# Low bits of the first layer's weights on VectorE, the second group's inversion alone on GpSimd, conversions placed behind its norms, ten weight loads ahead

## The chip, the cores and the metric

The kernel runs on one core of one Trainium2 chip. The metric is the device time of one execution in microseconds (us). Its engines are TensorE (PE; its weight loads are a row of their own, PEld), VectorE (DVE), ScalarE (ACT), GpSimd (POOL) and SyncE (SP), which here only issues DMA transfers. Each engine works through its own queue in order; semaphores tie the queues together.

## The reference

A linear attention with the delta rule, one time step after another, and then two feed-forward layers:

```python
k_n = k / (norm(k) + 1e-06)                    # q, k, v: 4 x 8 heads x 768 steps x 48
for t in range(768):
    y[t] = q[t] @ state
    state += beta[t] * outer(k_n[t], v[t] - k_n[t] @ state)
x = y as 3072 x 384
h = x @ w_in                                   # 384 x 2048
x = where(h >= 1, h, where(h <= -1, 0, (h + 1)**2 / 4)) @ w_out
h = x @ w_in2
out = max(h, 0)**2 @ w_out2
```

All in float32; the second layer's inputs and weights come with it, of the same sizes.

## The kernel before

**Tiling.** The 768 steps are cut into 24 chunks of 32. Per chunk the recurrence becomes matrix work: Gram matrices of keys and queries (`gram`), the inverse of a triangular matrix per head (`tri`), and products with the running state (`chunk_steps`: `ks`, `tr`, `qs`, `ku`, `pu`, `xt`). The triangular inverses are made for groups of chunks at a time, 2, 4, 4, 4, 4, 4, 2 of them. `tri` transposes the Gram tiles (`begin`, tile gm), computes norms and factors (`pre`), does a chain of dependent steps of two instructions each (`step`, L418 and L419, tiles t and tx), and transposes the result back (`end`, L422). For the first two groups only the two 16 x 16 diagonal halves are inverted in this way, in 14 steps; `joined` makes the block between them with PE products, for which `rows` (L452) transposes part of tx into a tile d (first group) or ld (second).

**Weights.** Products of 32-bit floats are made of parts: a weight is split into a rounded high part and a low part. The weights come as 64-bit values and are converted on the chip, in 32 tiles of 128 x 384 per layer. A conversion has these instructions: ACT scales the upper words into `wt` (L173, "prelu" in the code), the low bits are taken from the lower words into `wl` (L165), DVE joins the two (L183, "join"), ACT casts the high part (L194), and the low part is the difference of the two (L198, "difference"). For the first layer, L165 runs on POOL, and L198 on POOL for the input weights (i = 0) and on DVE for the output weights (i = 1). `wt` has 3 buffers and `wl` has 4. The raw weights of the first layer land in the buffers that later hold the converted ones. The second layer's conversions (on DVE, L165 too) are spread over the blocks of the first layer.

**Order.** The first part (loads, the first group's inversion, the second group's Gram tiles) is in the order in which the code writes it, on all engines. From `tc.manual_schedule(engines=ENGINES)` on only PE keeps the written order; the other queues are ordered by the scheduler, with its own cost model, under the limits of data, buffers and `issue_after`. The feed-forward stream then runs block after block (9 blocks of 2 or 3 chunks, 16 tiles f each, two slots per f), with a product h for tile f and the products into acc for tile f - 2. The attention work of the next chunks, the inversions and the conversions are put into slots of that stream (`put`, `put_a`, `HEAD`). `end1` and `rows1` of the second group are in slot 3 of the first block. SP issues transfers in order; a transfer whose buffer is not free holds those behind it.

**Names in the steps.** gp: Gram tiles of a group, later the inverse; l, ld, z: tiles of the second group's joining; kqt, kv: keys and queries, keys and values; raw: weights as they come; u, tr, ks, yy, xt: products of a chunk; sps and st: the running state in PSUM and SBUF; gh, gl: high and low part of the activated h. `first1(n)` issues the raw loads up to the n-th; `ahead` (L227 to L229) issues more as conversions go on; `more_w1` issues the next conversions.

Of the kernel before, what the change touches and what calls it, by code (L numbers as in the profile page):

```python
# [8 lines left out]
F32 = mybir.dt.float32  # L9
# [16 lines left out]
def kernel(  # L26
# [38 lines left out]
    EAGER = 26  # L65
# [6 lines left out]
    HEAD = 8  # L72
# [87 lines left out]
    def convert_stages(key, box, eng=None):  # L160
        eng = eng or nc.vector

        def low():
            box["t"] = tmp("wl", WL)
            eng.tensor_scalar(  # L165
                box["t"].bitcast(I32), box["raw"][:, :, 0].bitcast(U32), 2.0 ** -29, 7.0,
                ALU.mult, ALU.min,
            )

        def s0():  # L170
            raw = box["raw"] = raws.pop(key)
            t = box["w"] = tmp("wt", WT)
            nc.scalar.activation(  # L173
                t, raw[:, :, 1].bitcast(F32), AF.Prelu, scale=2.0 ** -112, alpha=2.0 ** 32
            )
            if eng is not nc.vector:
                low()

        def s1():
            if eng is nc.vector:  # L180
                low()
            t, bits = box["w"].bitcast(I32), box["t"].bitcast(I32)
            nc.vector.scalar_tensor_tensor(  # L183
                bits, t, 3, bits, ALU.logical_shift_left, ALU.bitwise_or
            )

        return [s0, s1]


    def part_stages(key, box):  # L190
# [5 lines left out]
        def s4():  # L196
            hi, lo = weight(i, f)
            (nc.vector if i else nc.gpsimd).tensor_sub(lo, box["t"], hi.bitcast(F32))  # L198

        return convert_stages(key, box, nc.gpsimd) + [s3, s4]  # L200
# [3 lines left out]
    def weight_items(w):  # L204
# [5 lines left out]
        def item(x):  # L210
            _, f, i = keys[x]
            box = {}
            if w == 0:
                r = part_stages(keys[x], box)
# [4 lines left out]
            r[1] = lambda: (s1(), ahead(x + 1 + RAW))  # L219
# [121 lines left out]
    def tri(n, eng, halves=False):  # L341
# [34 lines left out]
        def gamma2():  # L376
            nc.vector.scalar_tensor_tensor(r, g, -1.0, bet[:, n, :], ALU.mult, ALU.mult)
            nc.vector.tensor_mul(g, g, bet[:, n, :])
# [66 lines left out]
    def joined(n):  # L445
# [5 lines left out]
        def rows():  # L451
            nc.vector.transpose(d.rearrange("p q j -> p j q"), tx[:, 0:T2])  # L452
# [246 lines left out]
    with tc.manual_schedule():  # L699
# [3 lines left out]
        first1(2)  # L703
# [6 lines left out]
        first1(EAGER // 2)  # L710
        load_kv(HEADS)
        first1(EAGER)
# [22 lines left out]
        masks = [gram(0, 1, 2, late=2, eng=G)]  # L735
        cross_gram(0, 1)
        masks.append(gram(1, 1, 2, late=2, eng=G))
        for c in range(HEADS):
            save0(c)
        go([gram(c, late=2, eng=G) for c in range(GFIRST[1], GFIRST[2])])  # L740
        go(steps)
# [6 lines left out]
        begin()  # L748
    ENGINES = {mybir.EngineType.PE}
    with tc.manual_schedule(engines=ENGINES):  # L750
# [3 lines left out]
        go(pre)  # L754
# [5 lines left out]
        for fs in [[k0, t0], [k1], [q0, p0], [t1_], [q1], [x0], [p1], [x1]]:  # L760
            go(fs)
            more_w1(2)
# [45 lines left out]
        put(0, 3, *later(end1, rows1))  # L808
# [117 lines left out]
```

## Time and profile before

| | |
|---|---|
| median of 3 runs | 1098.58 us (1098.39 to 1100.24) |
| profiled execution | 1098.07 us |
| its span, first to last instruction | 1096.4 us |
| granted TensorE clock, mean | 0.976 of full speed |
| PE busy | 988.2 us, 90% of the span |
| DVE, ACT, POOL busy | 594.7, 513.4, 357.0 us |

The profile is one execution as the hardware profiler recorded it. A busy time counts the instructions of an engine, waits inside an instruction included; "idle before" and the name behind an arrow tell how long an engine had nothing running before an instruction and which work ended that. A matmul of 32-bit operands appears as two instructions or more. The chain of waits follows the last instruction back to what released it, step by step. The clock is that of TensorE alone, as a share of 2.4 GHz.

### The profile page before, as it was taken

Reading aid. Unit: us, or ns where it says so; the run is one execution under the profiler, and the core shown is the slowest. Engines: PE = TensorE matmul, PEld = TensorE weight load, DVE = VectorE, ACT = ScalarE, POOL = GpSimd, SP = SyncE. Lnnn points to the kernel's source line nnn. Section 1 sums busy time; section 2 is a strip of 40 time slices with the busy share of each in tenths; the row PEclk is TensorE's granted clock in tenths of the full one; section 3 lists DMA queues with packets and bytes.
Section 4 is the critical chain, followed back from the end, with each engine's and each line's share of the span. In section 5 each row is a group of like instructions: output and inputs, shape, how many; then the busy total and the mean of one; then the engine's idle time right before and its main releaser. Section 6 shows DMA issues by size and latency. Waiting matters only on the chain.

```text
span 1096.4 us, 34188 instructions
## 1 busy us (share of the span) xinstructions
PE 988.2 (90%) x14952; PEld 943.5 (86%) x14952; DVE 594.7 (54%) x1080; ACT 513.4 (47%) x1083; POOL 357.0 (33%) x474
## 2 busy tenths in 40 slices
PE   3340599899999999999999999999999999999998
PEld 3330588789989998999999999999999999999998
DVE  5662347767657666666755467743434343434333
ACT  3362246555555555565665666433333333333332
POOL 5989208618503921841940023210101010101000
PEclk9985799999999999999999999999999999999999
DMA  9910042534344144250212132301001010000000
GB/s 288 319 50 0 31 132 85 153 90 132 88 125 146 46 153 118 68 149 28 67 31 74 32 96 78 101 1 44 27 17 44 1 45 1 22 1 23 1 22 22
DMA packets 36054, 80.96 MB, mean 74 GB/s; under 512 B 4545, under 2 KB 18369, under 8 KB 35905
## 3 DMA queue, kind: packets, MB, share of 16 engines
q1 hardware_dynamic: 35904, 78.78, 23.6%
q8 instruction: 117, 1.92, 0.7%
q14 instruction: 33, 0.26, 0.1%
HBM read 63.03 MB, written 15.73 MB: 72 GB/s over the span
## 4 chain that ended last, share of the span: by engine, by line
PE 78%; DVE 7%; POOL 4%; issue 4%; DMA 3%; ACT 3%; SPq 0%; DVEq 0%; ACTq 0%; POOLq 0%
PE acc L574 34%; PE h L574 34%; POOL wl L165 2%; PE tr L505 2%; DMA raw<-in_w_dram 2%; PE sps L536 2%; PE g L289 2%; PE yy L491 2%; PE yy L525 1%; DVE g L603 1%; DMA kqt<-in_kq_dram 1%; PE ks L491 1%; POOL w L198 1%; ACT r L599 1%; DVE r L601 1%
## 5 line engine op out<-in xcount | busy, mean ns | idle before, releaser
L574 PE MATMUL h<-xh,w 128*128 128x384 f32 (+1 forms) x1632 | 319.6, 331 | 4.3 <-ACT g L600 3.4
L574 PEld LDWEIGHTS h<-xh,w 128*128 128x128 f32 x1632 | 270.9, 189 | 10.1 <-ACT g L600 2.5
L612 DVE TENSOR_TENSOR gl<-g,gh 128x384 fp32r<-128x384 f32 (+1 forms) x272 | 170.0, 625 | 144.1 <-ACT gh L611 141.6
L611 ACT CAST gh<-g 128x384 fp32r<-128x384 f32 (+1 forms) x272 | 134.5, 495 | 209.1 <-DVE g L603 103.8
L574 PE MATMUL h<-xl,w 128*128 128x384 f32 (+1 forms) x816 | 178.6, 327 | 1.1 <-DVE xl L562 1.1
L574 PE MATMUL acc<-gh,w 128*128 128x384 f32 (+1 forms) x864 | 166.6, 328 | 0.8 <-ACT gh L611 0.8
L606 DVE TENSOR_TENSOR g<-r 128x384 f32<-128x384 f32 x128 | 71.3, 557 | 157.8 <-ACT r L605 157.8
L574 PE MATMUL acc<-w,gh 128*128 128x384 f32 x768 | 155.5, 337 | 1.6 <-DVE e L619 1.6
L605 ACT ACTIVATE r<-h,zero 128x384 f32<-128x384 f32 x128 | 74.5, 582 | 166.7 <-PE h L574 166.7
L574 PEld LDWEIGHTS h<-xl,w 128*128 128x128 f32 x816 | 140.5, 189 | 1.7 <-DVE xl L562 1.7
L574 PEld LDWEIGHTS acc<-gh,w 128*128 128x128 f32 x864 | 135.2, 188 | 6.4 <-ACT gh L611 1.0
L574 PEld LDWEIGHTS acc<-w,gh 128*128 128x128 f32 x768 | 136.3, 188 | 1.9 <-ACT gh L611 1.9
L599 ACT ACTIVATE r<-h,one 128x384 f32<-128x384 f32 (+1 forms) x144 | 78.4, 545 | 84.3 <-PE h L574 83.4
L603 DVE TENSOR_TENSOR g<-g,r 128x384 f32<-128x384 f32 (+1 forms) x144 | 90.9, 631 | 42.7 <-ACT r L602 41.5
L601 DVE TENSOR_SCALAR r<-r 128x384 f32<-128x384 f32 (+1 forms) x144 | 64.8, 450 | 80.9 <-ACT r L599 80.0
L661 POOL CAST xh<-x2r 128x1152 fp32r<-128x1152 f32 x8 | 9.5, 1188 | 293.5 <-PE h L574 246.1
L418 POOL TENSOR_TENSOR t<-tx,gm 128x58 f32<-128x58 f32 (+9 forms) x164 | 94.8, 578 | 15.4 <-DVE tx L397 3.7
L419 POOL TENSOR_TENSOR tx<-tx,t 128x58 f32<-128x58 f32 (+9 forms) x164 | 95.5, 582 | 12.6
L574 PE MATMUL acc<-gl,w 128*128 128x384 f32 (+1 forms) x432 | 90.3, 317 | 0.0
L574 PE MATMUL acc<-w,gl 128*128 128x384 f32 x384 | 88.0, 337 | 0.0
L265 POOL TENSOR_TENSOR kv<-kv,nt 128x384 f32<-128x384 f32 x24 | 22.3, 931 | 201.3 <-DMA kv<-in_kv_dram 80.8
L602 ACT ACTIVATE r<-r 128x384 f32<-128x384 f32 (+1 forms) x144 | 70.5, 490 | 21.4 <-DVE r L601 20.8
(107 smaller groups left out, 1017.0 us busy)
## 6 DMA issues: line engine op xcount, KB each, us to landing
raw<-in_w_dram SPq DMA_DIRECT2D x64, 384.0 KB, 4.8
kqt<-in_kq_dram SPq DMA_DIRECT2D x88, 192.0 KB, 3.8
kv<-in_kv_dram SPq DMA_DIRECT2D x24, 384.0 KB, 3.1
w2f<-wl SPq DMA_DIRECT2D x32, 192.0 KB, 3.7
w2r<-w2f SPq DMA_DIRECT2D x16, 384.0 KB, 3.0
x2r<-x SPq DMA_DIRECT2D x8, 576.0 KB, 4.4
out_dram<-e SPq DMA_DIRECT2D x24, 192.0 KB, 2.0
x<-e SPq DMA_DIRECT2D x18, 192.0 KB, 2.5
```

The source lines that it names most:

```text
L418: eng.tensor_mul(t, by.to_broadcast(shape), of.to_broadcast(shape))
L419: eng.tensor_add(rest, rest, t)
L491: per_bh(lambda b, h, p, pd: nc.tensor.matmul(o[p, h], kqt[c][pd, b // 2, h, x * T:(x + 1) * T], st[pd, b // 2, h], start=h == 0, stop=x = ...
L574: nc.tensor.matmul(o, *((r, l) if swap else (l, r)), **flags)
L599: marks[0] = nc.scalar.activation(r, h, AF.Relu, bias=one)
L601: marks[1] = nc.vector.tensor_scalar(r, r, 2.0, 0.5, ALU.min, ALU.mult)
L602: nc.scalar.activation(r, r, AF.Square)
L603: nc.vector.tensor_add(g, g, r)
L605: marks[0] = nc.scalar.activation(r, h, AF.Relu, bias=zero)
L606: marks[1] = nc.vector.tensor_mul(g, r, r)
L611: nc.scalar.copy(ghi, g)
L612: nc.vector.tensor_sub(glo, g, ghi.bitcast(F32))
```

## The change

Four edits. (1) The low bits (L165) of the first layer's weights go from POOL to DVE, into the same stage as the join; of the differences (L198) of the input weights, those of the first 12 conversions go to DVE as well, the others stay on POOL. (2) `more_w1` calls of the hand-written part come under `issue_after` the last of the second group's factor instructions (the second line of `gamma2`), three steps of the conversion pipeline after each group of chunk products instead of two; the first part of that group's `pre` moves ahead, into the fully manual part. (3) The first two weights are no longer loaded ahead of the keys and values; ten are loaded ahead, and each conversion issues the load of the tenth after it, instead of 26 ahead and three. (4) The Gram tiles of the second group come ahead of the remaining ones of the first, `end1` and `rows1` move from slot 3 to 4, and `HEAD` from 8 to 10.

```diff
     LAG = 2
-    EAGER = 26
+    EAGER = 10
+    ALONE = 12
...
-    HEAD = 8
+    HEAD = 10
...
-    def convert_stages(key, box, eng=None):
-        eng = eng or nc.vector
-
-        def low():
-            box["t"] = tmp("wl", WL)
-            eng.tensor_scalar(
-                box["t"].bitcast(I32), box["raw"][:, :, 0].bitcast(U32), 2.0 ** -29, 7.0,
-                ALU.mult, ALU.min,
-            )
-
+    def convert_stages(key, box):
         def s0():
             raw = box["raw"] = raws.pop(key)
             t = box["w"] = tmp("wt", WT)
             nc.scalar.activation(
                 t, raw[:, :, 1].bitcast(F32), AF.Prelu, scale=2.0 ** -112, alpha=2.0 ** 32
             )
-            if eng is not nc.vector:
-                low()
 
         def s1():
-            if eng is nc.vector:
-                low()
-            t, bits = box["w"].bitcast(I32), box["t"].bitcast(I32)
+            raw, t = box["raw"], box["w"].bitcast(I32)
+            box["t"] = tmp("wl", WL)
+            bits = box["t"].bitcast(I32)
+            nc.vector.tensor_scalar(
+                bits, raw[:, :, 0].bitcast(U32), 2.0 ** -29, 7.0, ALU.mult, ALU.min
+            )
             nc.vector.scalar_tensor_tensor(
                 bits, t, 3, bits, ALU.logical_shift_left, ALU.bitwise_or
             )
...
-    def part_stages(key, box):
+    def part_stages(x, key, box):
...
         def s4():
             hi, lo = weight(i, f)
-            (nc.vector if i else nc.gpsimd).tensor_sub(lo, box["t"], hi.bitcast(F32))
-
-        return convert_stages(key, box, nc.gpsimd) + [s3, s4]
+            (nc.vector if i or x < ALONE else nc.gpsimd).tensor_sub(lo, box["t"], hi.bitcast(F32))
+
+        return convert_stages(key, box) + [s3, s4]
...
             s1 = r[1]
-            r[1] = lambda: (s1(), ahead(x + 1 + RAW))
+            r[1] = lambda: (s1(), ahead(x + 1 + (RAW if w else EAGER)))
...
         def gamma2():
             nc.vector.scalar_tensor_tensor(r, g, -1.0, bet[:, n, :], ALU.mult, ALU.mult)
-            nc.vector.tensor_mul(g, g, bet[:, n, :])
+            return nc.vector.tensor_mul(g, g, bet[:, n, :])
...
         nc.sync.dma_start(bet, beta)
-        first1(2)
         for c in range(GROUPS[0], KQ):
             load_kq(c)
         for c in range(KG):
             load_kg(KQ + c)
         for c in range(HEADS):
             load_kv(c)
-        first1(EAGER // 2)
+        first1(EAGER)
         load_kv(HEADS)
-        first1(EAGER)
...
         go(pre)
-        masks = [gram(0, 1, 2, late=2, eng=G)]
-        cross_gram(0, 1)
-        masks.append(gram(1, 1, 2, late=2, eng=G))
         for c in range(HEADS):
             save0(c)
         go([gram(c, late=2, eng=G) for c in range(GFIRST[1], GFIRST[2])])
+        cross_gram(0, 1)
+        masks = [gram(c, 1, 2, late=2, eng=G) for c in range(HEADS)]
         go(steps)
         for c in range(HEADS):
             value(c)
...
         begin, pre, steps, end1 = tri(1, G, True)
         begin()
+        ins = go(pre[:-2])
+        behind[0] = lambda: tc.issue_after(ins.ins)
     ENGINES = {mybir.EngineType.PE}
     with tc.manual_schedule(engines=ENGINES):
         for f in (ld0, dld0):
             for c in range(HEADS):
                 f(c)
-        go(pre)
+        go(pre[-2:])
...
         for fs in [[k0, t0], [k1], [q0, p0], [t1_], [q1], [x0], [p1], [x1]]:
             go(fs)
-            more_w1(2)
+            more_w1(3)
...
-        put(0, 3, *later(end1, rows1))
+        put(0, 4, *later(end1, rows1))
         for c in range(GROUPS[1]):
             put_a(0, HEAD - 3 + 3 * c, lambda c=c: ld1(c))
             put_a(0, HEAD - 2 + 3 * c, lambda c=c: dld1(c))
```

What it does to POOL's queue, around the second group's first steps. L418 and L419 are one step (t, then tx), L165 the low bits (wl), L198 the difference. Before:

```order
L198 TENSOR_TENSOR w07_1110<-wl_1093,w07_1110 128x384
L418 TENSOR_TENSOR t_732<-tx_80,gm_576 128x28
L165 TENSOR_SCALAR wl_1158<-raw_143 128x384
L198 TENSOR_TENSOR w08_1153<-wl_1115,w08_1153 128x384
L165 TENSOR_SCALAR wl_1187<-raw_145 128x384
L419 TENSOR_TENSOR tx_80<-tx_80,t_732 128x2x14
L165 TENSOR_SCALAR wl_1197<-raw_147 128x384
L165 TENSOR_SCALAR wl_1261<-raw_149 128x384
L198 TENSOR_TENSOR w09_1192<-wl_1158,w09_1192 128x384
L418 TENSOR_TENSOR t_736<-tx_80,gm_576 128x52
```

Now (L411 and L412 are the step):

```order
L376 TENSOR_TENSOR gm_544<-gm_544,st2_547 128x2x16x16
L385 TENSOR_TENSOR tx_80<-gm_544,st1_546 128x2x16x16
L411 TENSOR_TENSOR t_700<-tx_80,gm_544 128x28
L412 TENSOR_TENSOR tx_80<-tx_80,t_700 128x2x14
L411 TENSOR_TENSOR t_704<-tx_80,gm_544 128x52
L412 TENSOR_TENSOR tx_80<-tx_80,t_704 128x2x2x13
L411 TENSOR_TENSOR t_707<-tx_80,gm_544 128x72
L412 TENSOR_TENSOR tx_80<-tx_80,t_707 128x2x3x12
```

The steps stand one behind the other; the conversions between them are gone, and the differences that stay on POOL come behind the last step.

DVE's queue where it leaves the second group's factors (L378 before, L371 now) and starts on what follows. Before, with L183 the join, L501 a chunk's value minus its product, and L198 the difference:

```order
L374 TENSOR_TENSOR st1_578<-st2_579 128x32
L377 SCALAR_TENSOR_TENSOR st2_579<-st1_578,bet_75 128x32
L378 TENSOR_TENSOR st1_578<-st1_578,bet_75 128x32
L183 SCALAR_TENSOR_TENSOR wl_1020<-wt_1018,wl_1020 128x384
L501 TENSOR_TENSOR kv_109<-kv_109,ks_823 128x384
L183 SCALAR_TENSOR_TENSOR wl_1036<-wt_1034,wl_1036 128x384
L198 TENSOR_TENSOR w14_1080<-wl_1036,w14_1080 128x384
```

Now, with L173 the low bits, L176 the join, L191 the difference, L391 the copy of the diagonal into tx:

```order
L371 TENSOR_TENSOR st1_546<-st1_546,bet_75 128x32
L173 TENSOR_SCALAR wl_784<-raw_107 128x384
L173 TENSOR_SCALAR wl_793<-raw_109 128x384
L173 TENSOR_SCALAR wl_837<-raw_111 128x384
L173 TENSOR_SCALAR wl_847<-raw_113 128x384
L176 SCALAR_TENSOR_TENSOR wl_784<-wt_782,wl_784 128x384
L176 SCALAR_TENSOR_TENSOR wl_793<-wt_789,wl_793 128x384
L176 SCALAR_TENSOR_TENSOR wl_837<-wt_798,wl_837 128x384
L191 TENSOR_TENSOR w00_791<-wl_784,w00_791 128x384
L391 COPY tx_80<-st1_546 128x32
L176 SCALAR_TENSOR_TENSOR wl_847<-wt_842,wl_847 128x384
```

The conversions of four weights start directly behind the factors. From there to the second group's transposes there are 30 L173, 30 L176, 21 L191 and 12 others. The end of that stretch, now, with L415 and L445 the transposes of tx into gp and ld:

```order
L176 SCALAR_TENSOR_TENSOR wl_1330<-wt_1269,wl_1330 128x384
L191 TENSOR_TENSOR w112_1328<-wl_1266,w112_1328 128x384
L176 SCALAR_TENSOR_TENSOR wl_1352<-wt_1333,wl_1352 128x384
L173 TENSOR_SCALAR wl_1417<-raw_1153 128x384
L605 TENSOR_TENSOR gl_1215<-g_1208,gh_1214 128x256
L596 TENSOR_TENSOR g_1245<-g_1245,r_1244 128x256
L176 SCALAR_TENSOR_TENSOR wl_1417<-wt_1355,wl_1417 128x384
L191 TENSOR_TENSOR w113_1415<-wl_1352,w113_1415 128x384
L594 TENSOR_SCALAR r_1281<-r_1281 128x256
L415 STREAM_TRANSPOSE gp_245<-tx_80 128x32x32
L445 STREAM_TRANSPOSE ld_152<-tx_80 128x16x32
```

Before, the same place:

```order
L183 SCALAR_TENSOR_TENSOR wl_1648<-wt_1646,wl_1648 128x384
L198 TENSOR_TENSOR w112_1833<-wl_1648,w112_1833 128x384
L183 SCALAR_TENSOR_TENSOR wl_1739<-wt_1737,wl_1739 128x384
L183 SCALAR_TENSOR_TENSOR wl_1840<-wt_1838,wl_1840 128x384
L198 TENSOR_TENSOR w113_1954<-wl_1840,w113_1954 128x384
L183 SCALAR_TENSOR_TENSOR wl_1859<-wt_1857,wl_1859 128x384
L422 STREAM_TRANSPOSE gp_380<-tx_80 128x32x32
L452 STREAM_TRANSPOSE ld_184<-tx_80 128x16x32
```

In both orders the transposes stand behind the conversion of 30 weights; now the low bits are among them.

SP's queue at the last weights of the first layer. Before:

```order
L157 DMA raw_1735<-in_w1_dram 128x768
L141 DMA kv_1248<-in_kv_dram 128x768
L157 DMA raw_1855<-in_w1_dram 128x768
L141 DMA kv_1368<-in_kv_dram 128x768
L157 DMA raw_1836<-in_w1_dram 128x768
L132 DMA kqt_1693<-in_kq_dram 48x1024 x2
```

Now:

```order
L158 DMA raw_1153<-in_w1_dram 128x768
L158 DMA raw_1179<-in_w1_dram 128x768
L142 DMA kv_1320<-in_kv_dram 128x768
L158 DMA raw_1169<-in_w1_dram 128x768
L142 DMA kv_1408<-in_kv_dram 128x768
L133 DMA kqt_1764<-in_kq_dram 48x1024 x2
```

Each kv transfer there waits for a chunk's buffer. Before, the last weight stood behind two of them, now behind one.

## Rows read from the trace of the kernel before

**Rows 1.** The page, busy tenths in 40 equal slices, PE and POOL

```profile
PE   3340599899999999999999999999999999999998
...
POOL 5989208618503921841940023210101010101000
```

**Rows 2.** Busy time by stretch: PE, PEld, DVE, ACT, POOL, clock, DMA share, GB/s

```profile
80.00:100.00 20.00, 0.00 (x0) 0.00 (x0) 6.28 (x12) 6.79 (x14) 18.94 (x15) 0.50 0.00 0
```

**Rows 3.** Waits, 0 to 120 us: engine, line, releaser, total, times, longest

```profile
PE z L456 <- DVE ld L452: 45.0, 1, 45.0
```

**Rows 4.** Timeline, end of the second group's inversion: start, us, engine, line

```profile
105.09 0.36 POOL L418 TENSOR_TENSOR t<-tx,gm 128x100 f32<-128x100 f32 x1
...
110.77 0.33 POOL L418 TENSOR_TENSOR t<-tx,gm 128x88 f32<-128x88 f32 x1
...
113.76 2.01 DVE L422 STREAM_TRANSPOSE gp<-tx 128x1024 f32<-128x1024 f32 x1 [10.76 <-POOL tx L419]
115.68 0.98 DVE L452 STREAM_TRANSPOSE ld<-tx 128x512 f32<-128x512 f32 x1
```

**Rows 5.** Timeline of the first 50 us: loads, masks, norms

```profile
12.32 10.80 SPq L157 DMA_DIRECT2D raw<-in_w_dram  x11
...
20.88 0.55 ACT L173 ACTIVATE wt<-raw 128x384 f32<-128x384 f32 x1 [4.88 <-DMA raw<-in_w_dram]
...
27.69 1.28 POOL L304 TENSOR_TENSOR gp<-gp,mask 128x512 f32<-128x512 f32 x1
...
46.56 0.35 ACT L253 ACTIVATE st<-gm,tiny 128x32 f32<-128x32 f32 x1 [4.53 <-DVE gm L358]
...
48.79 0.49 DVE L378 TENSOR_TENSOR st<-st,bet 128x32 f32<-128x32 f32 x1
```

**Rows 6.** POOL's instructions by line, 0 to 120 us: count, busy, mean ns

```profile
L165 POOL TENSOR_SCALAR wl<-raw 128x384 int32<-128x384 uint32 x30 | 48.4, 1615 | 12.6 <-DMA raw<-in_w_dram 8.8 <-DVE w L198 1.7
L198 POOL TENSOR_TENSOR w<-wl,w 128x384 fp32r<-128x384 f32 x16 | 18.5, 1158 | 2.4 <-ACT w L194 1.4
...
L383 POOL TENSOR_TENSOR gm<-gm,st 128x512 f32<-128x512 f32 x1 | 1.3, 1274 | 0.0
```

**Rows 7.** Line 165 on DVE: duration in ns, least, median, most

```profile
L165 DVE TENSOR_SCALAR wl<-raw x32: 346/360/867, 184.6 to 533.5; 128x384 int32<-128x384 uint32 x32
```

**Rows 8.** Timeline, where DVE and POOL meet

```profile
24.09 0.55 DVE L198 TENSOR_TENSOR w<-wl,w 128x384 fp32r<-128x384 f32 x1
...
24.56 0.60 DVE L419 TENSOR_TENSOR tx<-tx,t 128x112 f32<-128x112 f32 x1
...
54.04 1.01 POOL L198 TENSOR_TENSOR w<-wl,w 128x384 fp32r<-128x384 f32 x1
54.33 1.14 DVE L183 SCALAR_TENSOR_TENSOR wl<-wt,wl 128x384 int32<-128x384 int32 x1
...
67.86 1.65 POOL L165 TENSOR_SCALAR wl<-raw 128x384 int32<-128x384 uint32 x1
...
68.59 0.56 DVE L198 TENSOR_TENSOR w<-wl,w 128x384 fp32r<-128x384 f32 x1 [0.47 <-ACT w L194]
...
83.46 0.56 DVE L183 SCALAR_TENSOR_TENSOR wl<-wt,wl 128x384 int32<-128x384 int32 x1 [2.49 <-POOL wl L165]
83.50 0.66 POOL L419 TENSOR_TENSOR tx<-tx,t 128x52 f32<-128x52 f32 x1
```

**Rows 9.** The chain of waits, 0 to 200 us: start, us, what

```profile
44.86 5.84 issue
...
117.85 2.22 PE h L574 x9
120.07 1.53 PE sps L536 x64
...
122.03 4.34 DMA raw<-in_w_dram
...
131.53 1.19 PE tr L505 x63
```

More of the change, by code (lines that the diff above doesn't have):

```diff
@@ L213, in item @@
             if w == 0:
-                r = part_stages(keys[x], box)
+                r = part_stages(x, keys[x], box)
             else:
@@ L451, in rows @@
         def rows():
-            nc.vector.transpose(d.rearrange("p q j -> p j q"), tx[:, 0:T2])
+            return nc.vector.transpose(d.rearrange("p q j -> p j q"), tx[:, 0:T2])
         def ld(c):
```

## The prediction, made before the result was known

> **What bounds the kernel now.** I read the page by slice first [rows 1]: a slice is 27.4 us. From the fifth on TensorE (PE) is full; in the third and fourth it has almost nothing to do, while GpSimd (POOL) is at 8 to 9 tenths. The room is in the first 135 us. The busy times by stretch [rows 2] sharpen that: in 80 to 100 us PE works 0.00 us, POOL 18.94 of 20, VectorE (DVE) 6.28, ScalarE (ACT) 6.79. The waits name the end of the hole: PE waited 45.0 us in one piece for the tile ld, which DVE transposes in L452 [rows 3]. The timeline at that place [rows 4] shows POOL in the last steps of the second group's inversion (L418, L419), undisturbed up to 113.7, then DVE's transposes (L422, L452) to 116.66, and only then PE. POOL is so late because 30 low-bit instructions (48.4 us) and 16 differences (18.5 us) stand between those steps [rows 6]. The time to watch is the end of ld, 116.66 us now.
>
> **When the norms are ready.** Before, ACT waits until 20.88 us for a weight that is the third of SP's queue [rows 5], and what stands behind it in ACT's queue is late. In the new SP order no weight stands ahead of the keys, so the first one comes two transfers earlier; eleven issues took 10.80 us, 0.98 each: 20.88 - 2 x 0.98 = 18.9, the next two 19.9 and 20.9. ACT's queue now mixes these three weights with the copies of the four Gram tiles and of l; the third weight (0.55) is done at 21.5, the second tile's mask on POOL (1.28 us) at about 22.5, and behind it come two rounds of an l copy, a Gram copy (I take 0.5 each, a little below the weight's 0.55) and a mask of 1.28: 22.5 + 2 x 2.28 = 27.1, with one mask held up 27.4 us. DVE's inversion of the first group no longer has conversions in it and is done before that. The transpose gm (2.0, as L422 of the same size) ends at 29.4; from there to the end of the norms the old trace took 46.56 to 49.28, 2.7 us, so 32.2 instead of 49.28. There the conversions may start.
>
> **What stands on DVE until the transpose.** The new DVE queue has 93 instructions between the norms and the second group's transpose: 30 low-bit ones (tensor_scalar), 30 joins (L183), 21 differences (L198) and 12 smaller ones. The low-bit one has a median of 0.36 us on DVE, where the second layer's weights already use it [rows 7], against 1.6 on POOL; join and difference have 0.55 to 0.56 [rows 8]. Back to back an operation of 0.55 costs 0.47, since the next starts before its end (24.09 to 24.56), and by the same overlap I take 0.28 for the 0.36. Alone: 30 x 0.28 + 51 x 0.47 + 4.6 = 37.0 us; with full durations 30 x 0.36 + 51 x 0.56 + 5.0 = 44.4.
>
> POOL works beside it: a value (no row of its own here; 1.0, as a difference of that size), gm and tx (1.27 each, tx taken as gm), 28 step instructions, and eight differences of 1.0 that come before the transpose. The last 20 steps ran from 105.09 to 113.76 undisturbed, and the last eight of these (from 110.77) have the sizes of the first eight: 8.7 + 3.0 = 11.7 us, at some 0.34 an instruction 9.6 of it busy [rows 4]. The two engines hinder each other [rows 8]. A DVE join that met a POOL difference (54.04, 1.01 us) took 1.14 and ended 0.42 after it; a POOL step that met a DVE join (83.46) took 0.66 and ended 0.14 after it, where even a wider step has 0.33 alone. Each waits for the other and saves 0.14 at the hand-over. It isn't so for every pair: the DVE difference at 68.59 ran in 0.56 in the middle of a POOL tensor_scalar. What is left on POOL in the new order are two-input operations alone, the kind that blocks. So I add for a step 0.20 + 0.42 - 0.47 = 0.15, 28 x 0.15 = 4.2; for a difference 0.87 - 0.05, 8 x 0.82 = 6.6; for the three others 0.87 + 1.13 + 1.13 - 0.15 = 3.0. The DVE stretch is 37.0 + 13.8 = 50.8 us.
>
> The Trainium skill, page "SBUF — State Buffer", section "Who interferes with whom", says that a VectorE instruction with two SBUF inputs and a GpSimd instruction that reads SBUF exclude each other for the whole instruction. The join of 1.14 agrees; the difference at 68.59 does not, since its partner read SBUF too. Taken to the letter, with nothing saved at a hand-over, the rule gives the first rival below, 1085 in place of 1067.
>
> ACT goes along: a cast and a weight, 1.0 to 1.1 us per weight at 0.55 the instruction, against about 1.5 on DVE; the differences stand mostly three or more places behind their joins, so the cast fits between. The wl ring of 4 lets DVE run to about the 98th place before it needs POOL's first difference, and that one the end of the steps: 28 at 0.62 after a start near 38, so at 56, about when DVE is there. For such small waits, and for a stall of PE's instruction issue in the first group's chain like the 5.84 us at 44.86 [rows 9] (ACT's copy u stands behind it in order, and casts behind u), I add 3.0, bounds 0 and 6. The transposes then begin at 32.2 + 50.8 + 3.0 = 86.0, and at 2.9 for the two ld is done at 88.9: 27.8 us sooner.
>
> **After ld.** Before, PE had h and the state product of the next step still to do, 2.22 + 1.53 us [rows 9], at the 0.50 of granted clock (1.2 GHz) that it had had in 80 to 100 us without work [rows 2]; with the move from slot 3 to 4 both come ahead of ld. Also before, the last weight stood in SP's queue behind a kv transfer, was issued at 122.03, took 4.34, held ACT until then, and the next tr of the chain came at 131.53, 14.9 after ld [rows 9]. In the new SP order the weight goes ahead of that kv; it still waits for the state product, so it lands some 4.7 after ld instead of 9.7. That is 0 to 6.8 us in all; I take 3, as HEAD = 10 pushes the next block's steps into 22 slots instead of 24 and can give some back. Later the orders of all queues are as before, and POOL, at 2 and 0 tenths in the fifth and sixth slice [rows 1], has time for the third group, so what is gained stays. The ten eager loads cost nothing: each conversion calls one ten ahead, at 0.98 us a load against the 1.5 of DVE.
>
> Sum: 27.8 + 3 = 30.8 off the profiled execution, which took 1098.07 (its span 1096.4 and 1.7 around it; the median is 0.5 more): 1067 us.
>
> **Rivals.**
> Full exclusion: every two-input operation of POOL adds its whole duration to DVE, 44.4 + 3.5 + 9.6 + 8.1 = 65.6; transposes at 32.2 + 65.6 + 3, ld at 103.7, 13.0 sooner: 1085. For it speaks the join of 1.14, against it the 0.14 saved at each meeting. Chance 0.2, with partial forms from 1077 on.
> No hindrance: DVE runs its 37.0 with no wait, ld at 72.1, 44.6 sooner, with what comes behind 1047 to 1054. For it speaks the difference at 68.59, against it that POOL keeps no tensor_scalar. 0.17.
> Slower, conversion by round trips: if DVE waited for the cast of each weight before going on, the transposes stand behind 29 whole trips over DVE, ACT and DVE. That decides from (113.76 - 32.2) / 29 = 2.8 us a trip on. One trip is 0.36 + 0.56 + 0.55 + 0.56 + 0.55, about 2.6; with POOL's difference in it 3.3: 32.2 + 29 x 3.3 = 128, 14 us later: 1112. For it: DVE was busy only 6.28 of 20 us where each weight went over three engines [rows 2]. Against it: the queue starts with four low-bit instructions ahead, and the rings hold three and four. 0.04.
> Hidden anyway: ld is early, but PE then waits as long for the last two weights or the third group, and nothing is left: 1097. The last weights hang on PE's own products, which come earlier too. 0.02.
>
> **How the numbers follow.** Forecast 0.57, 1059 to 1077 for its own terms (the 3.0 between 0 and 6, the 3 between 0 and 6.8, the hindrance by a third either way). The range for 8 in 10 reaches down into the case without hindrance, 1052, and up to most of full exclusion, 1083. Below 0.2%, 2.2 us, a measurement of this kernel cannot tell a change from none; faster 0.94 (forecast and both hindrance cases), same 0.02, slower 0.04.
>
> **What would show it.** Norms (L371 in the new file) ending near 32 us; L173 at about 0.36 where POOL is free; POOL's steps at 0.4 to 0.65 each with nothing between; the second group's transposes near 86; PE's hole ending near 89; the same picture from 200 us on, shifted. Wrong would be: DVE idle for ACT by more than 6 us between 32 and 86 (round trips), joins of over 0.8 us in the mean (full exclusion) or of 0.56 (none), or a later slice with less PE than before (given back).

## The result, and the profile after

The changed kernel takes 1064.06 us in the median of four runs (1060.89 to 1065.69), the kernel before 1098.49: ratio 0.968, 95% interval 0.965 to 0.971. Run once more beside later experiments it took 1062.01 in five runs (ratio 0.967, 0.966 to 0.968). So the gain is 34.4 to 36.4 us where 30.8 were forecast. The profiled execution is the fastest of the first four, 1060.89 us with a span of 1059.2, which is 37.2 less than before.

The page by slice, PE and POOL, answers to [rows 1]; a slice is now 26.5 us.

```profile
PE   4358898999999999999999998999999999999998
...
POOL 4641086184029308608700123110101010110000
```

In slices two to four POOL has 6, 4 and 1 tenths where it had 9, 8 and 9, and PE 3, 5 and 8 where it had 3, 4 and 0: the hole is filled from its end. Which engine is full instead stands in the busy times by stretch, the answer to [rows 2], with the same columns:

```profile
35.00:50.00 15.00, 3.80 (x194) 3.43 (x198) 14.71 (x27) 6.60 (x15) 12.61 (x24) 1.00 1.04 281
50.00:65.00 15.00, 7.58 (x306) 6.56 (x295) 14.10 (x31) 11.85 (x28) 7.52 (x10) 1.00 0.48 130
65.00:80.00 15.00, 9.78 (x100) 8.54 (x100) 14.16 (x30) 11.67 (x29) 6.61 (x6) 0.98 0.14 46
```

VectorE (third pair) works 14.1 to 14.7 of every 15 us. The bound has moved from POOL's queue to DVE's. DVE's timeline at the start and the end of the conversions gives the times that the prediction named, the answer to [rows 4, 5]:

```profile
34.49 0.19 DVE L371 TENSOR_TENSOR st<-st,bet 128x32 f32<-128x32 f32 x1
...
82.94 2.15 DVE L415 STREAM_TRANSPOSE gp<-tx 128x1024 f32<-128x1024 f32 x1
84.97 1.02 DVE L445 STREAM_TRANSPOSE ld<-tx 128x512 f32<-128x512 f32 x1
```

The norms end at 34.7 us (before 49.28, forecast 32.2), the transposes begin at 82.9 (forecast 86.0), and ld is done at 86.0 (before 116.66, forecast 88.9). PE's next tr, the end of the chain in [rows 9], starts at 95.00 instead of 131.53: 36.5 us sooner, which is all but 0.7 of the difference of the spans. From that tr on no more than this is given back or gained.

This holds for every kernel run here, which is how the experiments below are read. Each row is one profiled execution:

```
kernel                        norms   ld done  first tr after it   span   span - tr
before                         49.3    116.7        131.5        1096.4     964.9
after                          34.7     86.0         95.0        1059.2     964.2
after, second profile          35.0     88.1         97.4        1060.6     963.2
low bits alone                 72.0     97.6        108.1        1075.3     967.2
not queued behind the norms    72.6     99.1        108.8        1074.8     966.0
low bits back on POOL          34.1    122.3        132.0        1096.7     964.7
one step only                  33.2     90.7        100.3        1065.3     965.0
loads as before                34.5     87.1         97.7        1067.6     969.9
no difference on POOL          33.0     83.2         95.8        1058.0     962.2
the same, second profile       33.0     81.6         93.6        1058.7     965.1
some low bits on POOL          33.3     85.8        100.4        1064.8     964.4
half of the loads              33.6     85.2         94.1        1057.8     963.7
both of these                  33.3     81.5         93.6        1058.3     964.7
no difference, paced loads     33.3     79.1         90.7        1057.8     967.1
```

The last column lies between 962 and 970 without a pattern. The time is what tr starts at plus some 965, give or take 3 us in all rows but one, and a change of ld under 3 us can be seen in a profile but hardly in the time. The norms scatter too: the four rows "one step only", "no difference on POOL" (both profiles) and "some low bits on POOL" differ from the kernel after only in what comes behind the norms, and end them 1.4 to 2.0 us sooner than its two profiles.

### The profile page after: what moved, and what is told of

Its sections match the earlier page's. It is cut to its first block, busy times and chain, and to the rows that moved or that the text cites. A ratio compares the mean times of both kernels' runs of the same rounds, so it can differ in the third digit from the quotient of the medians.

```text
span 1059.2 us, 34189 instructions
## 1 busy us (share of the span) xinstructions
PE 995.1 (94%) x14952; PEld 948.8 (90%) x14952; DVE 607.8 (57%) x1119; ACT 512.6 (48%) x1083; POOL 302.6 (29%) x435
## 4 chain that ended last, share of the span: by engine, by line
PE 79%; DVE 9%; issue 4%; ACT 4%; POOL 2%; DMA 1%; SPq 0%; DVEq 0%; ACTq 0%; POOLq 0%
PE acc L567 35%; PE h L567 34%; DVE g L596 2%; PE g L282 2%; PE tr L498 2%; PE yy L484 2%; PE sps L529 2%; PE yy L518 1%; PE ks L484 1%; ACT r L592 1%; POOL w L191 1%; DVE gm L351 1%; ACT r L595 1%; ACT g L593 1%; DVE gl L605 1%
## 5 line engine op out<-in xcount | busy, mean ns | idle before, releaser
L411 POOL TENSOR_TENSOR t<-tx,gm 128x58 f32<-128x58 f32 (+9 forms) x164 | 97.1, 592 | 15.4 <-DVE tx L390 3.3
L412 POOL TENSOR_TENSOR tx<-tx,t 128x58 f32<-128x58 f32 (+9 forms) x164 | 94.8, 578 | 13.4 <-DVE tx L391 0.7
```

The costliest lines, as they stand in the source:

```text
L411: eng.tensor_mul(t, by.to_broadcast(shape), of.to_broadcast(shape))
L412: eng.tensor_add(rest, rest, t)
```

## Which part carries the gain

Theory A: POOL's 48.4 us of low bits [rows 6] stood between the steps of the second group's inversion, and moving them is the gain. Theory C: the new order (loads, masks, conversions queued behind the norms) is the gain, the low bits only change engine. Theory D: both are needed.

**Low bits alone** (the kernel before with the first part of the change, the low bits and the differences of the first twelve conversions; one place of the edit):

```diff
...
-        return convert_stages(key, box, nc.gpsimd) + [s3, s4]
+        return convert_stages(key, box) + [s3, s4]
```

> The kernel before with one part of the change alone: the low bits of the input weights on VectorE, the differences as in the kernel after (first twelve on VectorE). Loads, masks and the order of issue stay as before. In its VectorE queue 26 of the 30 conversions then stand ahead of the second group's norms (9 before, none after). Theory A (freeing GpSimd's 48.4 us of low bits is the gain; queueing the conversions behind the norms adds little): 26 conversions at 1.23 us alone and their hindrance, behind a first raw weight at 20.9 us and beside 13 us of first-group inversion, put the norms near 68 us, the 28 GpSimd steps at 0.56 us end near 85, ld is done at 86 to 93, time 1061 to 1071 us. Theory C (the loads, the masks and the queueing carry the gain, the low bits only change engine): ld stays above 105 us and the time above 1085. Theory D (both are needed, each worth about half): ld near 100, time 1075 to 1082.

Measured: 1075.89 us, ratio 0.979 (0.978 to 0.981), ld at 97.6. That is 22.7 us of the gain.

**Not queued behind the norms** (the kernel after without one line):

```diff
         ins = go(pre[:-2])
-        behind[0] = lambda: tc.issue_after(ins.ins)
```

> The kernel after with one part undone: the conversions are no longer issued behind the second group's norms, so 26 of them stand ahead of those norms in VectorE's queue; the low bits stay on VectorE, loads and masks as after. Theory A: norms near 65 us instead of 34.7, GpSimd's steps then end near 82 with VectorE's last four conversions beside them, ld at 85 to 90 against 86.0, time 1061 to 1068: the queueing is worth 0 to 5 us. Theory D (the queueing is worth half): ld near 100, time 1075 to 1082. If the meetings of GpSimd's steps with VectorE's conversions cost much, this kernel has fewer of them and could come out ahead of the kernel after: 1055 to 1060.

Measured: 1076.54 us, ratio 0.980 (0.978 to 0.981), ld at 99.1. The loads and masks, which this kernel has beyond the one above, bring nothing of their own without the queueing. The queueing is worth 12 to 14 us on top of the low bits, against the 0 to 5 of theory A. The timeline of DVE and POOL in this kernel shows why; the first row is the end of the norms, then the first and the last step on POOL.

```profile
72.44 0.19 DVE L371 TENSOR_TENSOR st<-st,bet 128x32 f32<-128x32 f32 x1
...
75.04 0.23 POOL L411 TENSOR_TENSOR t<-tx,gm 128x28 f32<-128x28 f32 x1
...
89.36 0.26 POOL L412 TENSOR_TENSOR tx<-tx,t 128x28 f32<-128x28 f32 x1
```

26 conversions run first, then the norms, then 14.6 us of steps with only four conversions left beside them. In the kernel after the same steps run from 37.3 to 53.1 under DVE's conversions, at a cost to DVE of 3.6 us (below). I had the norms at 65 to 68 and the transposes straight behind the steps; here they begin 6.3 us behind them, at 95.96. The kernel with the low bits alone shows the same: the last step ends at 88.8, but DVE's queue then holds operations of the feed-forward layers that wait for ScalarE, and the transpose L415 runs only at 94.02:

```profile
91.76 0.29 DVE L594 TENSOR_SCALAR r<-r 128x256 f32<-128x256 f32 x1 [1.93 <-ACT r L592]
...
94.02 2.13 DVE L415 STREAM_TRANSPOSE gp<-tx 128x1024 f32<-128x1024 f32 x1
```

**Low bits back on POOL** (the kernel after with the low bits alone undone; the differences of the first twelve conversions stay on DVE, so that POOL has 9 of them ahead of ld, not the 15 of the expectation):

> The kernel after with one part undone: the low bits of the input weights are back on GpSimd (and all its differences with them); loads, masks and the queueing behind the norms stay. Theory A: GpSimd again has 30 low bits at 1.6 us, 15 differences and 28 steps to do between 25 us and ld, about 48 + 16 + 12 us and its waits, so ld is done at 100 to 116 us and the time is 1075 to 1096. Theory C (loads, masks and queueing carry the gain): ld at 86 to 92 us, time 1062 to 1070.

Measured: 1097.98 us in ten runs, ratio 0.999 (0.998 to 1.000). Theory C falls: with the norms just as early the rest of the change gives nothing, less than even theory A allowed. POOL's timeline in this kernel:

```profile
39.85 0.23 POOL L419 TENSOR_TENSOR t<-tx,gm 128x28 f32<-128x28 f32 x1
40.17 3.09 POOL L166 TENSOR_SCALAR wl<-raw 128x384 int32<-128x384 uint32 x2
...
111.06 0.76 POOL L419 TENSOR_TENSOR t<-tx,gm 128x112 f32<-128x112 f32 x1
111.79 0.99 POOL L199 TENSOR_TENSOR w<-wl,w 128x384 fp32r<-128x384 f32 x1
...
119.10 0.26 POOL L420 TENSOR_TENSOR tx<-tx,t 128x28 f32<-128x28 f32 x1
```

The norms end at 34.1 and the first step runs at 39.9, but the steps again stand between low bits (L166) and differences (L199) until 113, and ld is done 5.6 us later than before. An early start of a chain is worth nothing while its engine serves another queue in between. POOL also stood idle there ahead of its low bits, 8.7 us for differences on DVE, which free their buffers, and 5.3 for raw weights. So the parts do not add up: the low bits alone bring 22.7, the queueing without them 0.6, both 34.4. Theory D in that sense holds. The order of the Gram tiles, the slots, HEAD and the place of the first twelve differences were not undone by themselves beside the queueing.

**Loads as before** (the kernel after with the old order of the raw loads):

```diff
-    EAGER = 10
+    EAGER = 26
...
+        first1(2)
...
```

> The kernel after with one part undone: the raw weights are loaded as before, two ahead of the later key tiles and 26 ahead in all, with no pacing. Theory A (of the 12.5 us that came with the queueing, none needs the loads): norms 1 to 3 us later than 34.7, ld at 85 to 90, time 1062 to 1068. Theory L (the masks' inputs wait for key tiles behind the weights, so that norms and conversions start late): norms at 40 or later, ld at 91 or later, time 1069 to 1076.

Measured: 1069.14 us (1064.92 to 1069.85), ratio 0.972 (0.970 to 0.974), ld at 87.1. By ld the loads are worth 1 us, as theory A has it; the median is 5 to 7 us up (4 to 5 by the ratios), and most of that lies behind tr (969.9 in the table, the highest there). Whether that belongs to the loads or to the scatter is not settled.

## What sets the end now

**One step only.** The second group's inversion on POOL is cut to its first of 14 steps, two instructions (the expectation speaks of two steps; the edit leaves one):

> The kernel after without 24 or more of the 28 GpSimd instructions of the second group's inversion: only its first two steps are left, so the second group's part of the result is not the reference's. It shows what those steps cost VectorE, whose queue sets ld. Partial hindrance as in the prediction (0.15 us per step, 4.2 in all): ld 3 to 5 us sooner, 81 to 83 us, time 1056 to 1061 beside 1061 to 1066. Full exclusion (GpSimd's step time of 15.8 us is taken from VectorE whole): ld 10 to 15 us sooner, 71 to 76. No hindrance: ld the same within 1 us.

```diff
-        steps = [lambda j=j: step(j) for j in range(1, (T2 if halves else T) - 1)]
+        steps = [lambda j=j: step(j) for j in range(1, (T2 if halves and n == 0 else 3 if halves else T) - 1)]
```

Measured: one run of 1066.99 us, ld at 90.7, later than with the steps, which none of the three expectations allowed. DVE's instructions by line (count, busy, mean ns of one, idle before and for whom), first in the kernel after beside the steps, 37.8 to 53.1 us, then here at 37 to 53:

```profile
L176 DVE SCALAR_TENSOR_TENSOR wl<-wt,wl 128x384 int32<-128x384 int32 x10 | 6.5, 662 | 0.0
L191 DVE TENSOR_TENSOR w<-wl,w 128x384 fp32r<-128x384 f32 x9 | 6.4, 710 | 0.3 <-ACT w L187 0.3
L173 DVE TENSOR_SCALAR wl<-raw 128x384 int32<-128x384 uint32 x8 | 3.8, 473 | 0.0
```

```profile
L176 DVE SCALAR_TENSOR_TENSOR wl<-wt,wl 128x384 int32<-128x384 int32 x8 | 4.3, 548 | 0.0
L191 DVE TENSOR_TENSOR w<-wl,w 128x384 fp32r<-128x384 f32 x7 | 3.9, 550 | 3.2 <-ACT w L187 3.2
L173 DVE TENSOR_SCALAR wl<-raw 128x384 int32<-128x384 uint32 x5 | 1.8, 351 | 0.0
L462 DVE TENSOR_TENSOR gp<-gp,w 128x128 f32<-128x128 f32 x2 | 0.6, 284 | 4.4 <-PE w L457 4.4
```

On DVE's own row the experiment is clean: each instruction is faster by 0.11 to 0.16 us without the steps, which over the 27 of the kernel after is 10 x 0.114 + 9 x 0.160 + 8 x 0.122 = 3.6 us, where 4.2 were predicted. The time did not follow, because DVE idled instead: 4.4 us for a product of PE that stands in DVE's queue among the conversions, and 3.2 for ScalarE (2.4 more behind 53 us). A second path, PE's first block, is about as long as DVE's queue. In this one execution it was longer than in the kernel after: PE's issue stood still for 4.00, 6.64, 5.58 and 5.17 us, there for 1.76, 6.09, 5.11 and 2.70 (second profile 1.76, 6.37, 5.58 and 4.62). How much of the later ld is scatter of that kind is open.

**Half of the loads.** What holds PE up in that block is the issue stall that I had priced with 3.0 us for DVE [rows 9]. The rivals on its cause are F, that PE's code comes through the DMA engines and waits there behind the weights, and N, that the stalls have nothing to do with the transfers.

```diff
+    lastraw = [None]
...
-        raw = raws[key] = pool.tile([P, DM, 2], I32, tag=tag, bufs=bufs, name="raw")
+        if w == 0 and x % 2 == 1:
+            raws[key] = lastraw[0]
+            return
+        raw = raws[key] = lastraw[0] = pool.tile([P, DM, 2], I32, tag=tag, bufs=bufs, name="raw")
```

> The kernel after with half of the input weights' loads left out: every second conversion takes the raw weight loaded for the one before it, so those weights are not the reference's; all instructions of the engines are the same. In the kernel after TensorE's issue stands still for 6.1, 5.1 and 2.7 us at 34 to 54 us, while the transfers fill 1.04 of the DMA engines. Theory F (TensorE's code comes through the same DMA engines and waits behind the weights): the three stalls shrink to under 2 us each, 10 us of them go; if VectorE's queue is nevertheless full from 34.7 us on, ld comes only 0 to 3 us sooner and the time is 1060 to 1064; if TensorE's first block sets ld with it, 5 us or more sooner and under 1060. Theory N (the stalls have nothing to do with the transfers): they stay at 5 to 6 us and the time at 1062 to 1067.

PE's timeline, first in the kernel after, then with half of the loads; in brackets is the idle time ahead.

```profile
32.53 1.52 PE L449 MATMUL z<-d,l 32*32 32x16 f32 x98 [1.76 <-issue]
33.84 0.60 PE L457 MATMUL w<-gp,z 32*32 32x16 f32 x30
40.53 1.51 PE L457 MATMUL w<-gp,z 32*32 32x16 f32 x97 [6.09 <-issue]
...
47.82 1.01 PE L498 MATMUL tr<-kv,gp 32*32 32x48 f32 x35 [5.11 <-issue]
...
54.23 0.93 PE L518 MATMUL yy<-u,gp 32*32 32x48 f32 x34 [2.70 <-issue]
```

```profile
36.77 1.51 PE L453 MATMUL z<-d,l 32*32 32x16 f32 x98 [5.91 <-issue]
...
41.48 1.51 PE L461 MATMUL w<-gp,z 32*32 32x16 f32 x97 [2.81 <-issue]
...
45.08 1.00 PE L502 MATMUL tr<-kv,gp 32*32 32x48 f32 x35 [1.47 <-issue]
...
47.60 1.50 PE L482 MATMUL ks<-u,cross 32*32 32x48 f32 x64 [1.51 <-ACT u L510]
```

And the DMA queues at 35 to 50 us (packets, MB, share of 16 engines), in the kernel after and in this one:

```profile
q1 hardware_dynamic: 1490, 4.17, 102.7%
q8 instruction: 2, 0.03, 0.9%
```

```profile
q1 hardware_dynamic: 572, 1.63, 47.0%
q8 instruction: 3, 0.05, 1.5%
```

With the transfers at less than half their share the two stalls of 6.09 and 5.11 us are 2.81 and 1.47, and the third is gone; the one of 5.91 (1.76 in the kernel after) still falls into the time of full transfers. So the stalls hang on the transfers, and N falls, though the first stays above the 2 us that F had. That it is PE's code that waits, as F has it, is borne out by where the stalls stand. The trace has a queue of its own for instructions, and over the whole run the page of the kernel after counts (packets, MB; then instructions):

```profile
q8 instruction: 117, 1.92, 0.8%
PE 995.1 (94%) x14952; PEld 948.8 (90%) x14952; DVE 607.8 (57%) x1119; ACT 512.6 (48%) x1083; POOL 302.6 (29%) x435
```

That is one packet of 16 KB for about every 256 of PE's products and weight loads. And the stalls stand at fixed places, before the same products of z, w and tr in both lists: the first two are 98 + 30 = 128 products apart, each with its weight load, the next two 127.

ld comes 0.8 us sooner and the time is 1059.42 us (ratio 0.964, 0.963 to 0.966). The norms were 1.1 us sooner here, so DVE's stretch from the norms to the transposes is as long as before, 48.4 us against 48.3, though 9.6 us of the three stalls are gone. In the profile of the kernel after, then, DVE's queue sets ld, and PE's block stands close behind it.

**No difference on POOL**, twice, the second time beside the kernel after:

```diff
-    ALONE = 12
+    ALONE = 32
```

> The kernel after with all differences ahead of ld on VectorE (those of the weights 12 to 29 on GpSimd go there too, 9 instructions). In the kernel after VectorE was blocked by them for about 7.5 us in 8 long instructions and two waits; as its own they cost 9 x 0.47 = 4.2 us. If VectorE's queue sets ld: ld 1 to 4 us sooner, time 1059 to 1064. If the blocking was less than it looked, or the queue waits elsewhere (for TensorE's first block): ld the same or up to 4 us later, time 1064 to 1069.

> The kernel after with all differences ahead of ld on VectorE, once more with more rounds. ld was done at 83.2 us against 86.0, its VectorE waited 3.3 us for TensorE's first block and 2.8 for ScalarE. If that is worth what ld shows: 2 to 3 us under the kernel after of the same call, 1060 to 1063. If the rest of the run scatters more than that: no difference outside 2 us.

> The kernel after once more, beside the three below on one chip: 1062 to 1066 us, ld at 85 to 87.

Measured: 1062.56 and 1061.12 us (ratios 0.9661 and 0.9657) against 1064.06 and 1062.01 of the kernel after. The first has an interval of 0.9645 to 0.9676, the second of 0.9644 to 0.967. ld comes at 83.2 and 81.6, against 86.0 and 88.1. But 1.7 and 1.9 us of that came with the norms, which the change does not touch. From the norms to the transposes DVE took 47.3 and 45.6 us, against 48.3 and 50.1: nine differences cost it 9 x 0.47 = 4.2 us of its own, and it waited 6.1 and 4.2 us for PE and ScalarE, so what they spare it in blocking is more than that. The second is 0.9 us under the kernel after beside it, where 2 to 3 were expected if ld counted in full, and that kernel's own ld of 88.1 lies a little outside its 85 to 87. The intervals overlap, so that it is faster than the kernel after is likely by this stretch and not shown by the time.

**Some low bits on POOL**: every second weight from the fourteenth on, in POOL's idle time.

```diff
+    LOWB = 14
...
-        return convert_stages(key, box) + [s3, s4]
+        return convert_stages(key, box, nc.gpsimd if x >= LOWB and i else None) + [s3, s4]
```

> The kernel after with the low bits of 8 of the 30 conversions ahead of ld (every second one from the fourteenth weight on) back on GpSimd, in whose row the 28 steps end at 53 us and half of the time to ld is idle. VectorE is rid of 8 x 0.55 = 4.4 us. Theory A (VectorE's queue sets ld, GpSimd has room): ld 2 to 4 us sooner, time 1059 to 1063. Theory G (a low bit of 1.6 us queued among the differences makes the joins wait): ld the same or later by up to 6 us, time 1064 to 1071.

Measured: 1065.12 us (ratio 0.969, 0.967 to 0.970), ld at 85.8. Nothing is gained: DVE waits 4.0 us for ScalarE's casts and 3.3 for PE. The numbers lie in the range of theory G, but no join waits for a low bit, which was its reason.

**No difference on POOL, and paced loads; both cuts together.**

```diff
-    EAGER = 10
-    ALONE = 12
+    EAGER = 18
+    ALONE = 32
...
+        q = nc.scalar if w == 0 and x >= EAGER else nc.sync
...
+            def paced():
+                s1()
+                with tc.issue_after(box["pre"].ins):
+                    ahead(x + 1 + RAW if w else max(EAGER + (x + 2) // 2, x + 4))
```

> All differences on VectorE, and the loads of the raw weights spread out: 18 ahead at once, then one from ScalarE's queue after every second conversion. The transfers then fill less than the 1.04 share of the DMA engines that they had at 35 to 57 us. Theory F (TensorE's code waits behind the weights, and its first block now holds VectorE up for 3.3 us): the stalls at 34 to 58 us shrink to 1 to 4 us each, ld at 79 to 83, time 1056 to 1061. If issuing from ScalarE or a late raw weight holds the conversions up: ld at 84 to 90, time 1063 to 1069.

> All differences ahead of ld on VectorE, and half of the input weights' loads left out (every second conversion takes the raw weight of the one before it, so those weights are not the reference's). Theory F: with neither GpSimd's differences nor TensorE's stalls in its way VectorE's queue runs full: ld 2 to 4 us sooner than the 83.2 of the kernel with the differences on VectorE alone, 79 to 81, and 4 to 6 sooner than the 85.1 of the kernel with the loads halved alone. If the two waits of VectorE are not TensorE's stalls but the conversions' own round trips: ld at 82 to 84.

Measured: paced 1062.35 us (1059.57 to 1066.99, ratio 0.968, 0.966 to 0.970), ld at 79.1, the earliest of all; both cuts 1060.15 us, ld at 81.5, between the two expected ranges and no sooner than the 81.6 without the cut loads, so the gain that theory F expected there did not come. In the paced kernel the transfers fill 0.87 of the DMA engines at 35 to 50 us, and one stall is still 5.82 us, against the 1 to 4 expected, the next is 3.94 and the third is gone. With ld 9.0 us sooner than in the second profile of the kernel after, measured beside it, the paced kernel's tr is only 6.7 sooner. PE's timeline in it says what comes last now:

```profile
80.63 0.71 PE L574 MATMUL acc<-gl,w 128*128 128x256 f32 x3 [3.15 <-DVE gl L612]
81.27 1.05 PE L456 MATMUL z<-ld,l 32*32 32x16 f32 x64
...
90.70 0.86 PE L505 MATMUL tr<-kv,gp 32*32 32x48 f32 x59
```

z, which needs ld, stands in PE's queue behind a product of the feed-forward stream, and that one waits for a DVE operation (gl) queued behind the transposes. The rest of its gain is lost behind tr (967.1 in the table), within the scatter. No version here beats the kernel after by more than the measurement can tell.

## Why the prediction was right, step by step

**What bounds the kernel** was right, and the two experiments on the low bits show it: POOL's queue decided. The page was read loosely: PE has 4 tenths in the third slice and 5 in the fifth and is full from the sixth on; nothing in the sum hangs on that.

**When the norms are ready** came 2.5 us late. The first weight was on ACT at 17.12 us (18.9 predicted), and the masks that gm needs were done at 25.1 (27.4). But "DVE's inversion of the first group [...] is done before that" failed: it was not free of POOL. The timeline of DVE and POOL in the kernel after:

```profile
18.97 0.27 DVE L411 TENSOR_TENSOR t<-tx,gm 128x112 f32<-128x112 f32 x1
19.28 1.30 DVE L412 TENSOR_TENSOR tx<-tx,t 128x112 f32<-128x112 f32 x1
...
29.01 0.99 DVE L445 STREAM_TRANSPOSE d<-tx 128x512 f32<-128x512 f32 x1
29.86 1.95 DVE L351 STREAM_TRANSPOSE gm<-gp 128x1024 f32<-128x1024 f32 x1
```

```profile
19.19 1.26 POOL L297 TENSOR_TENSOR gp<-gp,mask 128x512 f32<-128x512 f32 x1 [6.03 <-ACT gp L294]
```

A step of 0.27 us that meets a mask of 1.26 takes 1.30, and that happens three times (twice more with a value product), 4.1 us in all, so that gm, with its last mask done at 25.1, starts at 29.86 and not at 27.4. I had priced these meetings for the conversions and not for the stretch ahead of them. How many there are is luck of the execution. In the first profile with no difference on POOL, whose first part is the same, the first weight came where I had it,

```profile
18.90 0.55 ACT L165 ACTIVATE wt<-raw 128x384 f32<-128x384 f32 x1 [6.64 <-DMA raw<-in_w_dram]
```

and the norms still ended sooner, at 33.0, since only two steps met a mask (1.19 and 1.17 us).

**What stands on DVE** was mis-sized in its sum: 53.8 us predicted, 34.7 to 82.9 = 48.3 measured. The 37.0 for DVE alone is borne out where POOL is idle. In the second profile with no difference on POOL, by line at 56 to 79 us:

```profile
L191 DVE TENSOR_TENSOR w<-wl,w 128x384 fp32r<-128x384 f32 x17 | 9.5, 559 | 0.2 <-ACT w L187 0.2
L176 DVE SCALAR_TENSOR_TENSOR wl<-wt,wl 128x384 int32<-128x384 int32 x17 | 9.3, 558 | 0.0
L173 DVE TENSOR_SCALAR wl<-raw 128x384 int32<-128x384 uint32 x16 | 5.7, 361 | 0.0
```

34 x 0.47 + 16 x 0.28 = 20.5, and 2.5 for eight smaller ones at the same overlap, are 23.0, and from the first of them at 55.48 to the transpose at 78.59 DVE worked 22.9 us. So hindrance and waits together took 48.3 - 37.0 = 11.3 us, not 16.8. The steps' 4.2 was near (3.6 above). That leaves 7.7 us for the differences, the three others and all waits, priced at 6.6 + 3.0 + 3.0. The 3.0 for waits was hardly used: DVE waited 1.8 us for POOL, which belongs to the differences, and 0.3 for ScalarE, and PE's stalls stayed hidden under DVE's full queue. That they did was luck as well: in the second profile of the kernel after DVE waits 2.5 us for two casts that stand on ScalarE behind copies of PE's late products, the way I had priced it. In the kernel with no difference on POOL the stalls showed at once (3.3 and 2.9 us).

**The rivals.** Full exclusion would have joins of over 0.8 us; they took 0.58 in the mean (by line, 30 to 90 us, kernel after), and the 28 instructions of the steps, 9.6 us on POOL alone by [rows 4], cost DVE 3.6.

```profile
L176 DVE SCALAR_TENSOR_TENSOR wl<-wt,wl 128x384 int32<-128x384 int32 x31 | 17.6, 583 | 0.0
```

The Trainium skill, page "SBUF — State Buffer", section "Who interferes with whom", has one engine blocked for the whole instruction of the other: single meetings agree (1.30 above), the sum does not (3.6 for 9.6). No hindrance does not fall by that mean, which is close to the 0.56 named for it: most joins meet nothing. It falls by the rows beside the steps, where joins took 0.66 us against 0.55 without the steps. Round trips fall: DVE was busy 94 to 98%. Hidden anyway falls by the table.

**After ld** was mis-sized: 3 predicted within 0 to 6.8, tr 5.9 sooner behind ld measured (9.0 against 14.9). Both h and the state product are done ahead of ld, and PE works through without the wait for the last weight (busy times by stretch, columns as above):

```profile
86.00:95.00 9.00, 9.00 (x301) 8.32 (x301) 7.64 (x20) 7.00 (x19) 1.09 (x1) 0.98 0.28 91
```

But only part of that is owed to the new slots and the new order of loads: the low bits alone, with the old ones, have tr 10.5 behind ld, 4.4 of the 5.9. PE waits for no weight there either, although the last one is issued 3.5 us behind ld (before 5.4); why not was not followed.

The sum of the first terms was 27.8 for ld and came to 30.7, with 5.9 for 3: 36.5 to tr against 30.8. The errors of the norms (+2.5) and of the stretch (-5.5) partly cancelled.

## What to carry to other kernels

Price a move by the queue it empties, not by the engine's busy time: the same 48.4 us were worth 22.7 alone and 34 with the chain issued first, while issuing the chain first was worth nothing as long as its engine served another queue. When a bound goes, list what stands in order on the next engine, since here PE's first block, a few us shorter than DVE's queue, took over as soon as that got shorter. Read DVE's stretch and not only ld, since the norms ahead of it scatter by 2 us. Count meetings of two engines in every stretch, also the ones the change does not aim at.

## What the runs showed of the hardware

PE's issue stalls depend on the transfers of others: 6.09 and 5.11 us at a DMA share of 1.04 (35 to 50 us), 5.82 and 3.94 at 0.87, 2.81 and 1.47 at 0.49. The Trainium skill, page "Runtime: NRT & Kernel Launch", section "Instruction fetch mechanics", says that code is fetched in blocks of 16 KiB and the cost is mostly hidden; the packets agree in size (0.03 MB in two), the cost is not hidden here.

The granted clock of an idle PE is not the same in two executions. Without the queueing and with the low bits alone PE does nothing from 35 to 65 us (columns as above, first without the queueing):

```profile
35.00:65.00 30.00, 0.00 (x0) 0.00 (x0) 27.52 (x70) 17.66 (x39) 17.03 (x10) 0.50 0.68 169
```

```profile
35.00:65.00 30.00, 0.00 (x0) 0.00 (x0) 27.11 (x62) 17.19 (x38) 18.91 (x12) 1.00 0.56 167
```

One shows 1.2 GHz, the other 2.4. It is the execution rather than the kernel: the three other runs without the queueing have a mean granted clock of 0.994 to 0.995 over the whole run, the profiled one 0.964, and the four runs with the low bits alone 0.993 to 0.994. It cost nothing that can be measured, 1076.48 us against 1074.68 to 1077.52 in the other three. Why they differ stays open.
